# Queries loaded and turned first, w1 loaded ahead of an exchange, and two tiles of an expert begun early, in a fused attention and expert kernel

## The chip, the cores and the metric

The kernel runs on one core of a Trainium2 chip. The metric is the device time of one execution in microseconds; lower is better. Engines go by their names and by the short names of the profile: TensorE (PE), VectorE (DVE), ScalarE (ACT), GpSimd (POOL) and SyncE (SP).

## The reference

Two stages, one behind the other, in float32:

```python
def _attn_ref(q, k, v, sort_net):          # (4, 8, 768, 64) each; sort_net (4, 8, 8, 8)
    P = sort_net
    for _ in range(5):                     # exp, then rows and columns normalized
        P = P - np.max(P, axis=-1, keepdims=True)
        P = np.exp(P)
        P = P / (np.sum(P, axis=-1, keepdims=True) + 1e-09)
        P = P / (np.sum(P, axis=-2, keepdims=True) + 1e-09)
    k_sorted = np.einsum('bhij,bhjcd->bhicd', P, k_b)    # blocks of 96 rows mixed by P
    v_sorted = np.einsum('bhij,bhjcd->bhicd', P, v_b)
    scores = scale * np.matmul(q_b, k_sb.transpose(0, 1, 2, 4, 3))   # within each block
    attn = softmax(scores)
    return np.matmul(attn, v_sb)

def _moe_ref(x, w_gate, w1, w2):           # x (3072, 512), 8 experts, F = 1024
    P = np.exp(x @ w_gate - max)           # then balanced over rows and columns 8 times
    for e in range(8):
        out += P[:, e:e + 1] * (np.maximum(x @ w1[e], 0.0) @ w2[e])
```

The attention's output, with its heads side by side, is the x of the second stage.

## The kernel before, in words

The four batches of the attention are worked one after the other. While batch 1, 2 or 3 is in the attention, expert 0 runs on the tokens of the batch before it, woven between (`weave`). Behind the last batch come the balancing of the gates and experts 1 to 7, which fill most of the time. The part that the change touches is the opening: everything up to batch 0's attention, and the first tiles of expert 0.

**Loads.** `load_batch`, `load_rest`, `load_w1` and `load_w2` issue their DMAs from GpSimd (L75, L84, L89), which also turn float32 into bfloat16. They are issued in the order of the text: q, v and k of heads 0 to 3 of batch 0, the same of heads 4 to 7, v of batch 1 (768 KB in bfloat16), the gate's weights wg (L97). w1 and w2 of expert 0 and batch 1's k and q follow behind the exchange.

**The chain of P.** `sort_net` is loaded on SP (L60). Five rounds of one Exp on ACT (L118) and six or seven small instructions on DVE (L119 to L126) balance P. `Prep` (L130) is P repeated, which PE spreads over the partitions (L389), and DVE multiplies with a mask (L393) to the matrices R by which blocks are mixed.

**Batch 0.** `queries` turns the queries on PE (L178) and copies them on ACT (L190). `sort_values` multiplies v with R (L155), copies the result to vs (L157), and then exchanges partitions: eight DMAs of 97.5 KB (L165) take vs in SBUF to vsb in SBUF, one for each block. They are shared out over SP, ACT and GpSimd. Behind that, `attention` follows a written plan, in which a letter is a step and a digit a pair of heads:

```python
plan = ("k0 k1 w3 s0 q2 k2 w2 s1 q3 k3 d0 w1 s2 w2 d1 s3 d2 w1 m0 m1 d3 t0 v0 w1 m2 t1 "
        "w1 m3 t2 v0 w2 t3 l0 w3 l3" if first else
```

- q: `queries`. k: `keys`, the mixed keys (L200), copied on DVE (L205). s: `scores` (L219) and their Exp on ACT (L232).
- d: `denominators` (L243) and a reciprocal on DVE (L246). m: `mix`, attention times vsb (L255), multiplied with the reciprocals on DVE (L258). m0 is the first reader of vsb.
- t: `turn`, the output turned (L278) and copied to xtT, x turned (L281). l: `logits` with wg (L292), copied to glog (L296).
- v0: two heads of batch 1's `sort_values`. w with a digit: `warm`, so many matmuls (L381) into a bank of PSUM that nothing reads.

PSUM has seven banks here that go round, and one for the unread matmuls.

**Expert 0.** `expert` makes hidden tiles (L336, ReLU on ACT L338), eight for each chunk of 384 tokens, and then multiplies with w2 (L343). Batch 0's first chunk starts behind the plan's last step. Between its steps stand the other four heads of batch 1's `sort_values`, and behind these batch 1's exchange.

`pin` keeps instructions of an engine in the order of the text. A scheduler places those without it.

Of the kernel before, what the change touches and what calls it, by code (L numbers as in the profile page):

```python
# [25 lines left out]
def kernel(  # L26
# [31 lines left out]

    P = pp.tile([32, 8, 8], F32)
    nc.sync.dma_start(out=P, in_=sort_net.rearrange("b h i j -> (b h) i j"))  # L60

# [3 lines left out]
    def load_batch(bb, parts):  # L67
        for d, name in ((vt, "vt"), (kt, "kt"), (qt, "qt")):
            d[bb] = kvp.tile([128, 8, 384], BF16, name=name, bufs=2)
        load_rest(bb, parts)  # L70
# [19 lines left out]
                                in_=moe_w2[e].rearrange("(fb k) f -> k fb f", k=128)))  # L90

    Ibig = ones.tile([128, 128], BF16)
    make_identity(nc, Ibig)
    load_batch(0, [(x, l0, 4) for l0 in (0, 4) for x in "qvk"])
    load_batch(1, [("v", 0, 8)])
    wg = ones.tile([128, 4, E], BF16)
    pin(nc.gpsimd.dma_start(out=wg, in_=moe_w_gate.rearrange("(kk k) e -> k kk e", k=128)))  # L97
    mask16 = ones.tile([128, 16], F32)
    nc.vector.reduce_sum(out=mask16, in_=Ibig.rearrange("p (j c) -> p c j", c=16), axis=AX.X)

# [9 lines left out]
    rs = pp.tile([32, 8], F32)  # L110
    cs = pp.tile([32, 8], F32)
    Pt = P.rearrange("p i j -> p j i")
    nc.vector.reduce_max(out=rs, in_=P, axis=AX.X)
    nc.vector.tensor_sub(P, P, mkap(rs, [rs.ap[0], rs.ap[1], [0, 8]]))
    for it in range(5):


        nc.scalar.activation(out=P, in_=P, func=AF.Exp)  # L118
        nc.vector.reduce_sum(out=rs, in_=P, axis=AX.X)  # L119
        nc.vector.reciprocal(out=rs, in_=rs)  # L120
        nc.vector.tensor_mul(P, P, mkap(rs, [rs.ap[0], rs.ap[1], [0, 8]]))
        nc.vector.reduce_sum(out=cs, in_=Pt, axis=AX.X)
        if it == 0:
            nc.vector.tensor_scalar_add(cs, cs, 1e-9)
        nc.vector.reciprocal(out=cs, in_=cs)
        nc.vector.tensor_mul(Pt, Pt, mkap(cs, [cs.ap[0], cs.ap[1], [0, 8]]))  # L126

    Prep = perp.tile([32, 8, 8, 16], BF16)
    for eng, i0, n in ((nc.vector.tensor_copy, 0, 5), (nc.scalar.copy, 5, 3)):
        eng(Prep[:, i0:i0 + n], mkap(P, [P.ap[0], [8, n], [1, 8], [0, 16]], off=i0 * 8))  # L130

    xtT = xtp.tile([128, 4, N], BF16)
    osbl = xtp.tile([128, NT, Dm], F32)
    glog = xtp.tile([128, NT, E], F32)
    Pb = perp.tile([128, 32, 8], F32)
    Rt = {}

# [14 lines left out]
    def sort_values(bb, bank, n=8, h0=0):  # L152
        for h in range(h0, n):
            vps = bank([128, 384], F32)
            pin(nc.tensor.matmul(vps, Rt[bb][:, h].rearrange("p i c -> p (i c)"),  # L155
                                 vt[bb][:, h, :], start=True, stop=True))
            (nc.vector.tensor_copy if bb == 0 and h in (3, 5, 7) else nc.scalar.copy)(  # L157
                vs[:, :, h, 0:64], vps.rearrange("p (kk d) -> p kk d", d=64))
            if h % 2:
                yield  # L160

        for i in range(NB if n == 8 else 0):
            eng = ((nc.sync, nc.gpsimd, nc.scalar)[i % 3] if bb == 0 else
                   nc.gpsimd if i % 2 else nc.sync)
            (pin if bb == 0 else lambda ins: ins)(eng.dma_start(  # L165
                out=mkap(vsbt[bb % 2], [[VW, 96], [1, 520]], off=i * 520),
                in_=vs[16 * i:16 * i + 16].rearrange("p kk h d -> p kk (h d)")))
# [3 lines left out]
    def queries(bb, hp, bank):  # L171

        qps = bank([128, 6, 128], BF16)
        if bb < 2:

            for kk in range(6):
                for h in range(2):
                    pin(nc.tensor.matmul(qps[64 * h:64 * h + 64, kk, :],  # L178
                                         qt[bb][:, 2 * hp + h, kk * 64:kk * 64 + 64],
                                         Ibig, is_transpose=True, start=True, stop=True))  # L180
        else:
            qr = sp.tile([128, 6, 2, 64], BF16, name="qr", bufs=2)
            nc.gpsimd.tensor_copy(
                qr.rearrange("p kk h d -> p h kk d"),
                qt[bb][:, 2 * hp:2 * hp + 2].rearrange("p h (kk d) -> p h kk d", d=64))
            for kk in range(6):
                pin(nc.tensor.matmul(qps[:, kk, :], qr[:, kk].rearrange("p h d -> p (h d)"),  # L187
                                     Ibig, is_transpose=True, start=True, stop=True))
        qT[bb, hp] = sp.tile([128, 128, 6], BF16, name="qTs", bufs=4)
        nc.scalar.copy(qT[bb, hp], qps.rearrange("p kk c -> p c kk"))  # L190

    def keys(bb, hp, bank):

# [104 lines left out]
    def attention(bb, bank, values=None, warm=None):  # L298
        first = bb == 0

        def step(what, hp):
            if what == "q":
                queries(bb, hp, bank)
            elif what == "k":
                keys(bb, hp, bank)
            elif what == "s":
                scores(bb, hp, bank)
            elif what == "t":
                turn(bb, hp, bank, nc.scalar.copy if first and hp < 3 else nc.vector.tensor_copy)
            elif what == "l":  # L310
                logits(bb, bank, (0, 1, 2) if hp == 0 else (3,))
            elif what == "v":
                next(values, 0)
            elif what == "w":
                warm(hp)
            elif what == "d":
                denominators(hp, bank)
            else:
                for h in range(2):
                    mix(bb, hp, h, bank)  # L320

        plan = ("k0 k1 w3 s0 q2 k2 w2 s1 q3 k3 d0 w1 s2 w2 d1 s3 d2 w1 m0 m1 d3 t0 v0 w1 m2 t1 "
                "w1 m3 t2 v0 w2 t3 l0 w3 l3" if first else
                "q0,q1,k0 k1,s0,q2 k2,s1,q3 m0 k3,s2 m1,t0 s3 m2,t1 m3 t2 t3,l0 l3")
        for some in plan.split():
            for x in some.split(","):
                step(x[0], int(x[1]))
            yield


    def expert(e, c0, n, hsb, hbank, obank, done, hold):
        hTs = hsb()
        for fb in range(8):
            hps = hbank()
            for kk in range(4):
                hold(nc.tensor.matmul(hps[:, 0:n], w1t[e][:, kk, fb * 128:(fb + 1) * 128],  # L336
                                      xtT[:, kk, c0:c0 + n], start=(kk == 0), stop=(kk == 3)))
            nc.scalar.activation(out=hTs[:, fb, 0:n], in_=hps[:, 0:n], func=AF.Relu)  # L338
            yield
        for tt in range(n // 128):  # L340
            oacc = obank()
            for fb in range(8):
                hold(nc.tensor.matmul(oacc, hTs[:, fb, tt * 128:(tt + 1) * 128],  # L343
                                      w2t[e][:, fb, :], start=(fb == 0), stop=(fb == 7)))
                if fb == 3:
                    yield
            done(c0 // 128 + tt, oacc)
            yield
# [23 lines left out]
    with tc.tile_pool(name="ps0", bufs=7, space=bass.MemoryType.PSUM,  # L372
# [8 lines left out]
                pin(nc.tensor.matmul(unread, Ibig, mkap(Ibig, [Ibig.ap[0], [0, 4], [1, 128]]),  # L381
                                     start=True, stop=True))

        for hp in range(2):
            queries(0, hp, bank0)
        warm(9)
        pbps = bank0([128, 8, 32], F32)
        for i in range(8):
            pin(nc.tensor.matmul(pbps[:, i, :], Prep[:, i].rearrange("p j c -> p (j c)"),  # L389
# [10 lines left out]
        nc.scalar.copy(Pb, pbps.rearrange("p i g -> p g i"))  # L400
        half = build_r(1, nc.gpsimd, 4)
        next(half)
        load_w1(0)
        next(half, 0)
        load_w2(0)
        load_rest(1, [(x, l0, 4) for l0 in (0, 4) for x in "kq"])
        for _ in attention(0, bank0, sort_values(1, bank0, 4), warm):
            pass

    def weave(a, b, na, nb):  # L410
# [8 lines left out]
    with ExitStack() as c2:  # L419
# [4 lines left out]
        for bb in range(1, B):  # L424
            ex = expert0(bb - 1, lambda: mps.tile([128, 8, 384], BF16, name="hTs"),
                         ebank, ebank, pin)
            at1, left = attention(bb, bank1), 12 if bb == 1 else 26
            late = sort_values(1, bank1, 8, 4) if bb == 1 else iter(())
            for _ in range(28 - left):
                next(ex)  # L430
                next(late, 0)
            last = 3 if bb + 1 < B else 0
            left -= last
            cut = lambda k: left * k // 12
            weave(at1, ex, 5, cut(5))
            if bb + 1 < B:
                if bb == 2:
                    load_w1(1)
                load_batch(bb + 1, [(x, 0, 8) for x in "vkq"])
                for _ in build_r(bb + 1, nc.gpsimd, 4):  # L440
                    pass
                if bb == 2:
                    for _ in sum_w(1):
                        pass
            weave(at1, ex, 3, cut(8) - cut(5))
            if bb + 1 < B:
                weave(sort_values(bb + 1, bank1), ex, 5, last)
            weave(at1, ex, 4, left - cut(8))
            for _ in ex:
                pass  # L450
# [401 lines left out]
```

## Time and profile before

| | us |
|---|---|
| three timed executions | 675.99, 674.03, 676.01 |
| their median | 675.99 |
| the profiled execution | 674.6 |
| its span | 672.8 |
| PE busy in the span | 658.8 |
| HBM read, written | 52.45 MB, 6.29 MB |

The span runs from the first to the last instruction; 1.8 us of the profiled execution lie around it. All times in a view are counted from the span's start. Busy shares are those of the engines' queues, and a matmul's end in the timeline is modelled, so that matmuls overlap there; the start of the next group tells more than the length of one.

### The profile page before, as it was taken

The numbers are of one execution on the slowest core, as the hardware profiler recorded it, in microseconds if no ns is written. First come the engines' busy times: TensorE is split into PE (matmuls) and PEld (weight loads), VectorE is DVE, ScalarE is ACT, GpSimd is POOL, SyncE is SP. The second block draws the span as 40 slices with busy tenths as digits, with TensorE's granted clock in tenths as the row PEclk, the third lists the DMA queues.
The fourth block names the chain that finished last, engine by engine and source line by source line (L and its number), as shares of the span: only waits on it lengthen the run. The fifth ranks groups of instructions, "written<-read, shape, count | busy, mean of one in ns | idle before, by whom it ended". The sixth has DMA issues, their size and how long they took to land.

```text
span 672.8 us, 13418 instructions
## 1 busy us (share of the span) xinstructions
PE 658.8 (98%) x5185; PEld 436.0 (65%) x5185; DVE 470.2 (70%) x957; ACT 380.0 (56%) x738; POOL 470.0 (70%) x437
## 2 busy tenths in 40 slices
PE   5999999999999999999999999999999999999997
PEld 2756666654566666666666666666666666666665
DVE  6627646667677777777777777777777777777775
ACT  3656646466777755555555555555555555555540
POOL 4442651076979998779796979879787969846641
PEclk9999999999999999999999999999999999999999
DMA  9996872203040313030403040211303040000224
GB/s 154 195 221 102 155 123 33 33 1 63 1 64 3 62 10 55 1 63 0 64 1 63 1 63 2 37 28 12 53 0 63 1 64 1 1 1 35 92 86 166
DMA packets 31968, 36.57 MB, mean 54 GB/s; under 512 B 2016, under 2 KB 24384, under 8 KB 31904
## 3 DMA queue, kind: packets, MB, share of 16 engines
q0 software_dynamic: 26352, 27.72, 26.2%
q1 hardware_dynamic: 5328, 7.80, 3.6%
q8 instruction: 40, 0.66, 0.4%
q10 hardware_dynamic: 224, 0.20, 0.1%
q14 instruction: 24, 0.20, 0.1%
HBM read 52.45 MB, written 6.29 MB: 87 GB/s over the span
## 4 chain that ended last, share of the span: by engine, by line
PE 95%; DVE 2%; ACT 1%; issue 0%; DMA 0%; ACTq 0%; DVEq 0%
PE oacc L674 37%; PE bk L563 37%; PE bank L343 5%; PE bank L336 5%; PE bank L267 1%; PE bk L640 1%; PE oacc L739 1%; PE bank L219 1%; PE bank L200 1%; PE bank L278 1%; PE bk L731 1%; PE bank L155 1%; PE unread L381 1%; PE bk L739 1%; PE oacc L731 0%; PE bank L187 0%
## 5 line engine op out<-in xcount | busy, mean ns | idle before, releaser
L624 DVE SCALAR_TENSOR_TENSOR osbl<-oacc,glog,osbl 128x256 f32<-128x256 f32 (+1 forms) x410 | 219.1, 535 | 127.2 <-PE oacc L674 118.0
L549 ACT ACTIVATE hT<-bk 128x512 bf16<-128x512 f32 (+1 forms) x176 | 104.3, 592 | 148.6 <-PE bk L563 129.8
L563 PE MATMUL bk<-xtT,w1e 128*128 128x512 bf16 x504 | 149.1, 379 | 0.0
L674 PEld LDWEIGHTS <-hs 128*128 128x128 bf16 x984 | 96.2, 98 | 63.0 <-POOL hs L664 0.3
L674 PEld LDWEIGHTS <-hT 128*128 128x128 bf16 x904 | 88.4, 98 | 59.0 <-issue 1.8
L664 POOL TENSOR_TENSOR hs<-hT 128x512 bf16<-128x512 bf16 x82 | 94.9, 1157 | 36.5 <-DVE hT L552 31.1
L674 PE MATMUL oacc<-w2e,hT 128*128 128x256 bf16 x764 | 114.6, 273 | 0.3 <-DVE osbl L624 0.3
L664 POOL TENSOR_TENSOR hs<-hs,hT 128x512 bf16<-128x512 bf16 x82 | 94.8, 1156 | 6.4
L563 PE MATMUL bk<-xc,wc 128*128 128x512 bf16 x336 | 99.1, 379 | 0.1
L664 POOL TENSOR_TENSOR hs<-hT,hs 128x512 bf16<-128x512 bf16 x82 | 94.6, 1154 | 6.4
L674 PE MATMUL oacc<-w2e,hs 128*128 128x256 bf16 x616 | 92.4, 273 | 0.0
L563 PEld LDWEIGHTS <-w1e 128*128 128x128 bf16 x672 | 65.8, 98 | 11.7 <-issue 0.5
L552 DVE CUSTOM_DVE_ANT_0 hT<-bk,p 128x512 bf16<-128x512 f32 x84 | 58.1, 691 | 7.9 <-PE bk L563 3.1
L598 ACT COPY p<-bk 128x512 f32<-128x512 f32 x84 | 49.2, 586 | 24.8 <-PE bk L563 24.7
L592 ACT COPY u<-bk 128x512 f32<-128x512 f32 x84 | 49.3, 586 | 22.1 <-PE bk L563 22.0
L583 ACT COPY bk<-bk 128x512 f32<-128x512 f32 x84 | 48.0, 572 | 20.5 <-PE bk L563 20.5
L552 DVE CUSTOM_DVE_ANT_0 hT<-bk,u 128x512 bf16<-128x512 f32 x84 | 57.0, 679 | 1.0 <-PE bk L563 0.6
L674 PE MATMUL oacc<-w2s,hs 128*128 128x256 bf16 x368 | 55.2, 273 | 0.0
L563 PEld LDWEIGHTS <-wc 128*128 128x128 bf16 x504 | 49.3, 98 | 8.0 <-issue 0.2
L617 DVE SCALAR_TENSOR_TENSOR s<-bk,hT 128x512 bf16<-128x512 f32 x80 | 54.4, 680 | 0.0
L563 PE MATMUL bk<-xc,w1e 128*128 128x512 bf16 x168 | 50.0, 379 | 0.1
L563 PE MATMUL bk<-xtT,wc 128*128 128x512 bf16 x168 | 50.0, 379 | 0.0
(140 smaller groups left out, 853.0 us busy)
## 6 DMA issues: line engine op xcount, KB each, us to landing
w1e<-in_moe_w_dram POOLq DMA_DIRECT2D x8, 1024.0 KB, 8.1
w2e<-in_moe_w_dram POOLq DMA_DIRECT2D x8, 1024.0 KB, 8.9
out_dram<-osbl SPq DMA_DIRECT2D x23, 256.0 KB, 2.0
vt<-in_v_dram POOLq DMA_DIRECT2D x3, 768.0 KB, 11.9
qt<-in_q_dram POOLq DMA_DIRECT2D x4, 384.0 KB, 12.8
kt<-in_k_dram POOLq DMA_DIRECT2D x4, 384.0 KB, 13.4
kt<-in_k_dram POOLq DMA_DIRECT2D x2, 768.0 KB, 14.4
qt<-in_q_dram POOLq DMA_DIRECT2D x2, 768.0 KB, 16.5
```

What stands on the lines that cost most here:

```text
L336: hold(nc.tensor.matmul(hps[:, 0:n], w1t[e][:, kk, fb * 128:(fb + 1) * 128], xtT[:, kk, c0:c0 + n], start=(kk == 0), stop=(kk == 3)))
L343: hold(nc.tensor.matmul(oacc, hTs[:, fb, tt * 128:(tt + 1) * 128], w2t[e][:, fb, :], start=(fb == 0), stop=(fb == 7)))
L549: relu = lambda o, x: nc.scalar.activation(out=o, in_=x, func=AF.Relu)
L552: return nc.vector._custom_dve(TENSOR_ADD_SAT, out=o, in0=x, in1=y, s0=TOP, s1=0.0)
L563: pin(nc.tensor.matmul(ps, wa[:, kk, :], xa[:, kk, :], start=(first and kk == 0), stop=(kk == 1), skip_group_check=True))
L583: pin(nc.scalar.copy(t["w"], t["u"]))
L592: pin(nc.scalar.copy(t["u2"], t["u"]))
L598: pin(nc.scalar.copy(t["p5"], t["v"]))
L617: pin(nc.vector.scalar_tensor_tensor(out=s3[:, i, :], in0=t["w"], scalar=0.0, in1=c12, op0=ALU.max, op1=ALU.subtract))
L624: pin(nc.vector.scalar_tensor_tensor(out=o, in0=ps, scalar=glog[:, t, e:e + 1], in1=o, op0=ALU.mult, op1=ALU.add))
L664: pin(nc.gpsimd.tensor_tensor(out=s[:, c], in0=a, in1=b, op=o))
L674: pin(nc.tensor.matmul(ps, h[:, fb, :], w[:, fb, :], start=(first and fb == 0), stop=(fb == 3), skip_group_check=True))
```

## The change

It does the following.

- The first load is q of heads 0 to 3, ahead of the identity matrix `Ibig`; then q of heads 4 to 7, then v and k of heads 0 to 3 and of 4 to 7.
- w1 of expert 0 is loaded behind them, in the place of batch 1's v, which is now issued between the two parts of batch 1's R, behind the exchange.
- The gate's weights are loaded on SP as float32, behind `sort_net`, into a part of glog that is not in use yet, and a copy on GpSimd makes wg of them.
- All four pairs of heads of batch 0's queries are turned before P is ready, pinned between the Exps of the chain of P: two, then four unread matmuls, then the other two and three unread matmuls. Nine unread matmuls stood there.
- The exchange has four DMAs on SP, two on ACT and two on GpSimd. For batch 0 there were three, two and three.
- The plan of batch 0 has no q steps, ten unread matmuls where there were sixteen, m0 ahead of d2, and no steps of batch 1's `sort_values`. All eight heads of these now stand between expert 0's first tiles, with half of their copies on DVE.
- Steps e0, e1 and e2 (`begin`) make the first two hidden tiles of expert 0 inside the plan, a part of the contraction at a time, as the parts of xtT are done. `expert` leaves those two out.

```diff
+    wgf = glog[:, NT - 4:NT, :]
+    nc.sync.dma_start(out=wgf, in_=moe_w_gate.rearrange("(kk k) e -> k kk e", k=128))
...
+    load_batch(0, [("q", 0, 4)])
     make_identity(nc, Ibig)
-    load_batch(0, [(x, l0, 4) for l0 in (0, 4) for x in "qvk"])
-    load_batch(1, [("v", 0, 8)])
+    load_rest(0, [("q", 4, 4)] + [(x, l0, 4) for l0 in (0, 4) for x in "vk"])
+    load_w1(0)
     wg = ones.tile([128, 4, E], BF16)
-    pin(nc.gpsimd.dma_start(out=wg, in_=moe_w_gate.rearrange("(kk k) e -> k kk e", k=128)))
+    pin(nc.gpsimd.tensor_copy(wg, wgf))
...
-            (nc.vector.tensor_copy if bb == 0 and h in (3, 5, 7) else nc.scalar.copy)(
+            (nc.vector.tensor_copy if bb == 0 and h in (3, 5, 7) or bb == 1 and h % 2 else
+             nc.scalar.copy)(
...
-            eng = ((nc.sync, nc.gpsimd, nc.scalar)[i % 3] if bb == 0 else
-                   nc.gpsimd if i % 2 else nc.sync)
+            eng = (nc.sync if i % 2 == 0 else
+                   nc.scalar if bb == 0 and i % 4 == 1 else nc.gpsimd)
...
-        plan = ("k0 k1 w3 s0 q2 k2 w2 s1 q3 k3 d0 w1 s2 w2 d1 s3 d2 w1 m0 m1 d3 t0 v0 w1 m2 t1 "
-                "w1 m3 t2 v0 w2 t3 l0 w3 l3" if first else
+        plan = ("k0 k1 w3 s0 k2 w2 s1 k3 w2 d0 s2 d1 s3 w1 m0 d2 m1 d3 t0 m2 t1 m3 e0 t2 w2 t3 "
+                "l0 e1 l3 e2" if first else
...
+    def begin(bank, ks):
+
+        if not begun:
+            begun[0] = mps.tile([128, 8, 384], BF16, name="hTs")
+            begun[1] = [bank([128, 384], F32) for _ in range(2)]
+        for fb in range(2):
+            for kk in ks:
+                pin(nc.tensor.matmul(begun[1][fb], w1t[0][:, kk, fb * 128:(fb + 1) * 128],
+                                     xtT[:, kk, 0:384], start=(kk == 0), stop=(kk == 3)))
+            if 3 in ks:
+                nc.scalar.activation(out=begun[0][:, fb], in_=begun[1][fb], func=AF.Relu)
+
...
-        for hp in range(2):
-            queries(0, hp, bank0)
-        warm(9)
...
+            pin(nc.scalar.activation(out=P, in_=P, func=AF.Exp))
+            if it >= 2:
+                queries(0, it - 2, bank0)
+            if it == 3:
+                warm(4)
...
+        queries(0, 3, bank0)
+        warm(3)
...
-        load_w1(0)
+        load_batch(1, [("v", 0, 8)])
...
-        for _ in attention(0, bank0, sort_values(1, bank0, 4), warm):
+        for _ in attention(0, bank0, iter(()), warm):
...
-            late = sort_values(1, bank1, 8, 4) if bb == 1 else iter(())
-            for _ in range(28 - left):
+            late = sort_values(1, bank1) if bb == 1 else iter(())
+            for _ in range(28 - left - 2 * (bb == 1)):
```

More of the change, by code (lines that the diff above doesn't have):

```diff
@@ L60 @@
     nc.sync.dma_start(out=P, in_=sort_net.rearrange("b h i j -> (b h) i j"))
+    xtT = xtp.tile([128, 4, N], BF16)
+    osbl = xtp.tile([128, NT, Dm], F32)
+    glog = xtp.tile([128, NT, E], F32)
+    wgf = glog[:, NT - 4:NT, :]
+    nc.sync.dma_start(out=wgf, in_=moe_w_gate.rearrange("(kk k) e -> k kk e", k=128))
     pin = tc.keep_in_program_order
@@ L112 @@
     Pt = P.rearrange("p i j -> p j i")
[L113 to L126, printed above, removed]
-    Prep = perp.tile([32, 8, 8, 16], BF16)
[L129 to L134, printed above, removed]
+    Prep = perp.tile([32, 8, 8, 16], BF16)
     Pb = perp.tile([128, 32, 8], F32)
@@ L189, in queries @@
         qT[bb, hp] = sp.tile([128, 128, 6], BF16, name="qTs", bufs=4)
-        nc.scalar.copy(qT[bb, hp], qps.rearrange("p kk c -> p c kk"))
+        (pin if bb == 0 else lambda ins: ins)(
+            nc.scalar.copy(qT[bb, hp], qps.rearrange("p kk c -> p c kk")))
     def keys(bb, hp, bank):
@@ L317, in step @@
                 denominators(hp, bank)
+            elif what == "e":
+                begin(bank, ((0, 1), (2,), (3,))[hp])
             else:
@@ L328, in attention @@
             yield
+    begun = {}
+    def begin(bank, ks):
[8 more added lines that the diff above has]
+                nc.scalar.activation(out=begun[0][:, fb], in_=begun[1][fb], func=AF.Relu)
     def expert(e, c0, n, hsb, hbank, obank, done, hold):
-        hTs = hsb()
-        for fb in range(8):
+        hTs = begun[0] if c0 == 0 else hsb()
+        for fb in range(2 if c0 == 0 else 0, 8):
             hps = hbank()
@@ L382, in warm @@
                                      start=True, stop=True))
-        for hp in range(2):
-            queries(0, hp, bank0)
-        warm(9)
+        nc.vector.reduce_max(out=rs, in_=P, axis=AX.X)
+        nc.vector.tensor_sub(P, P, mkap(rs, [rs.ap[0], rs.ap[1], [0, 8]]))
+        for it in range(5):
+            pin(nc.scalar.activation(out=P, in_=P, func=AF.Exp))
[3 more added lines that the diff above has]
+                warm(4)
+            nc.vector.reduce_sum(out=rs, in_=P, axis=AX.X)
+            nc.vector.reciprocal(out=rs, in_=rs)
+            nc.vector.tensor_mul(P, P, mkap(rs, [rs.ap[0], rs.ap[1], [0, 8]]))
+            nc.vector.reduce_sum(out=cs, in_=Pt, axis=AX.X)
+            if it == 0:
+                nc.vector.tensor_scalar_add(cs, cs, 1e-9)
+            nc.vector.reciprocal(out=cs, in_=cs)
+            nc.vector.tensor_mul(Pt, Pt, mkap(cs, [cs.ap[0], cs.ap[1], [0, 8]]))
+        for eng, i0, n in ((nc.vector.tensor_copy, 0, 5), (nc.scalar.copy, 5, 3)):
+            (pin if i0 else lambda ins: ins)(
+                eng(Prep[:, i0:i0 + n], mkap(P, [P.ap[0], [8, n], [1, 8], [0, 16]], off=i0 * 8)))
+        queries(0, 3, bank0)
+        warm(3)
         pbps = bank0([128, 8, 32], F32)
```

## The prediction

> **What bounds the kernel now.** I read the page first, then the timeline of the first 60 us, the chain of waits, the DMA issues one by one, and the windows. The page:
>
> ```profile
> span 672.8 us, 13418 instructions
> PE 658.8 (98%) x5185; PEld 436.0 (65%) x5185; DVE 470.2 (70%) x957; ACT 380.0 (56%) x738; POOL 470.0 (70%) x437
> ```
>
> TensorE (PE) is busy 98% of the span. From 33 us on its idle stretches are short, so whatever PE finishes earlier up to there reaches the end, and nothing else does. The change touches only the first 40 us. The timeline (start, length, engine, line):
>
> ```profile
> 10.36 0.15 PEld L381 LDWEIGHTS <-Ibig 128*128 128x128 bf16 x1 [0.28 <-issue]
> 10.79 0.15 PEld L381 LDWEIGHTS <-Ibig 128*128 128x128 bf16 x1 [0.28 <-issue]
> 11.11 0.10 PEld L381 LDWEIGHTS <-Ibig 128*128 128x128 bf16 x1 [0.18 <-issue]
> ...
> 12.92 0.36 PE L389 MATMUL bank<-Ibig,Prep 32*128 32x32 bf16 x8 [1.22 <-DVE Prep L130]
> ...
> 17.93 0.53 PE L178 MATMUL bank<-Ibig,qt 128*64 128x128 bf16 x12
> ...
> 25.30 1.59 PE L255 MATMUL bank<-vsb,atp 96*96 96x88 bf16 x32
> ...
> 33.28 0.81 PE L336 MATMUL bank<-xtT,w1e 128*128 128x384 bf16 x4
> ...
> 39.13 5.34 PE L343 MATMUL bank<-w2e,hTs 128*128 128x512 bf16 x24
> ```
>
> Until 12.9 us PE only waits for the chain of P on VectorE and ScalarE (Prep, L130). From there it is nearly gapless, but part of what it runs is unread matmuls (L381). Two marks serve below: the first mix at 25.30 (m0, L255, reads vsb) and the first w2 matmul at 39.13. The unread ones start every 0.43 us until about 11.0 us and then faster; in the chain of waits (start, length, what) they take 0.22 us:
>
> ```profile
> 20.26 0.46 PE bank L178 x12
> 32.62 0.67 PE unread L381 x3
> 35.07 0.33 PE bank L155 x2
> 35.39 3.90 PE bank L336 x24
> ```
>
> So PE runs at half rate until about 11 us; the PEclk column reads 1.00 throughout and does not show it. The DMA issues, asked one at a time (KB, then us to landing; in order k's second half, v of batch 1, the exchange's first and last piece on SP, w1):
>
> ```profile
> kt<-in_k_dram POOLq DMA_DIRECT2D x1, 384.0 KB, 11.1
> vt<-in_v_dram POOLq DMA_DIRECT2D x1, 768.0 KB, 14.4
> vsb<-vs SPq DMA_DIRECT2D x1, 97.5 KB, 4.6
> vsb<-vs SPq DMA_DIRECT2D x1, 97.5 KB, 6.8
> w1e<-in_moe_w_dram POOLq DMA_DIRECT2D x1, 1024.0 KB, 11.7
> ```
>
> With the issue times (5.31, 6.04, 16.52, 17.9, 19.71) they land at 16.4, 20.4, 21.1, 24.7 and 31.4. The windows (PE, PEld, DVE, ACT, POOL busy, PEclk, DMA share, GB/s) say why:
>
> ```profile
> 5.00:15.00 10.00, 6.96 (x51) 3.62 (x52) 7.62 (x32) 3.45 (x9) 2.72 (x4) 1.00 1.31 203
> 15.00:19.00 4.00, 3.80 (x71) 2.30 (x69) 3.66 (x8) 2.49 (x7) 1.88 (x4) 1.00 1.32 204
> 21.00:22.00 1.00, 1.00 (x22) 0.81 (x17) 0.99 (x2) 1.00 (x4) 1.00 (x2) 1.00 1.06 293
> ```
>
> DMA is saturated at 203 GB/s by the GpSimd queue from 5 us. The exchange, issued from 16.5, moves nothing before 19 us and its first piece lands only after v of batch 1 did. It is complete 0.6 us before m0 needs it.
>
> **The change, part by part.** *Chain of P.* Order of instructions: on VectorE the mask reduction (L99, 0.36 us) now stands between a column sum and its reciprocal inside the third iteration; before, it ran at 6.84 while VectorE waited for an Exp. Cost about 0.3 on the path (0 if it slips, 0.4 at most). On ScalarE three copies of turned queries (0.77 each) now stand behind Exps; the wait for VectorE there is 1.55 us per iteration, so they are covered as long as q's first half lands before about 7.5. It landed at 6.8 and is issued 0.7 earlier (ahead of the identity, 0.74 instead of 1.46). If it came later than 7.5, the Exp behind the copy, and all of P, would slip by as much. w_gate moves to SP behind P's load, where nothing follows until the exchange; its cast on GpSimd stands ahead of two exchange issues and waits for a load that is long done. Zero.
>
> *Removed from PE between 12.9 and 39.1.* 24 transposes (0.36 + 0.42 by start times; now done while PE waits for P): 0.8. Unread matmuls of the attention plan 16 to 10: 6 x 0.22 = 1.3. Nine unread ahead of P's matmuls become four plus three: beside the wait for Prep, 0. Gaps of PE between 17 and 34 that the early expert matmuls may fill: 0.3. Four v matmuls (0.65) move behind, eight expert matmuls (1.3) move ahead of the last logits: both stay before 39.13, 0. Upper bound of the gain: 0.8 + 1.3 + 0.3 - 0.3 = 2.1 us.
>
> *When m0 can start.* On PE alone: 25.30 less 0.8 (transposes), 0.65 (three unread), 0.74 (the denominators d2, now behind m0), plus 0.3: 23.4. Exps on ScalarE, back to back from 18.25 to 25.88 with two copies (about 0.6 each) among them, end near 25.0; only d3, later, needs the last. But the exchange now stands behind w1 instead of v. w1 follows k's second half: 15.7 (0.7 earlier), plus 1024 KB, 5.2 us at 203 GB/s or 6.3 at the 167 GB/s of 72 to 79 us, where another w1 load runs: landing 20.9 to 22.0, against 20.7 for w_gate's, last in that queue before the exchange. So the exchange is 0.2 to 1.3 later, 0.75 in the middle; w_gate's small rows no longer stand in the queue, some 0.5 back. Last piece 24.7 + 0.25 = 24.95; as it is read seventh of eight (0.045 apart), m0 behaves as if it began at 24.65. PE idles there about a microsecond: the unread matmuls and transposes that went were partly cover for this wait, and d2, which could fill it, is queued behind m0.
>
> *From m0 to 39.13.* Before: 13.8 us. After: five unread fewer (1.1), d2 more (0.74): 13.5, and VectorE's eight products (0.62 each) leave no more to win. The gain is 25.30 - 24.65 + 0.3 = 0.95, say 1.0.
>
> *Later covers.* w2 landed at 36.5 (21.56 + 14.9), needed at 39.1 and now 38.1; the queue has the same bytes ahead of it. q of batch 1 landed at 45.7 (24.73 + 21.0), needed at 48.5, now 47.5. v of batch 1 comes about 29, needed about 33. Its copies, half now on VectorE, run beside PE.
>
> [...] The row: the exchange's SP piece took 4.6 us, and P's load, alone, 1.7. [...]
>
> **Rivals.**
> - A, the forecast: m0 waits a little for the exchange; gain 1.0.
> - B, the exchange is not held: it lands before 23.7 and m0 starts at 23.4; gain 1.9 + 0.3, held to the upper bound of 2.1: 672.5. For it: only two pieces remain behind w1 on GpSimd's queue. Against: the 4.6 us.
> - C, slower: v of batch 1, issued about 19.4, is served while SP's four pieces wait, so the last ones come a v load later (4.0 us by 16.4 to 20.4). Landing 21.5 + 4.0 and two pieces of about 1 us: 27.6, m0 at 27.3; loss 1.7, 676.3. It turns to a loss when the last piece lands after 25.9. For it: SP now has four pieces in a row. Against: w1 behind the old exchange did not hold it so long.
> - D, the clock: PE comes to P's matmuls at half rate, since 9 unread in a row became 4, transposes, 3. Four unread then cost 0.86 more, eight v matmuls 1.3 more; with the rest hidden by VectorE some 2 us later, so a net loss of about 1.0: 675.6. Against: transposes began the busy stretch before too, and PE was fast 4.2 us after they began.
> - E, nothing: 674.6; a later wait (w2, q) takes it all back.
>
> [...]
>
> **How the numbers follow.** The sum is made against the profiled execution, 674.6 (span 672.8 and 1.8 around it): 673.6. The four executions shown (674.0, 674.6, 676.0, 676.0) average 675.2, 0.6 above it; I add half of that: 673.9. The median of before is 675.99, and 0.3% of it, about what a measurement of this kernel can tell from no change, is 2.0, itself the spread of before. So A falls on both sides of the bound 673.96. Chances: A 0.46 (0.24 faster, 0.21 same, 0.01 slower), B 0.24 (0.22, 0.02, 0), C 0.14 (0, 0.08, 0.06), D 0.11 (0, 0.07, 0.04), E 0.05 (0.01, 0.04, 0). Sums: faster 0.47, same 0.42, slower 0.11. Range: B's 672.5 less the 0.6 by which the lowest run of before is under its profiled one, 671.9, to C's 676.3 plus the 1.4 by which the median of before exceeds its profiled run, 677.7; 677.5 leaves little out.
>
> **What would show it.** After: the first matmul on queries near 6.1; unread loads 0.43 or 0.22 apart at 11 to 13.5; Prep's matmuls at 13.2; m0 at 23.4 to 24.7 with a PE wait on vsb of about 1 us in it; first w2 matmul at 38.1. A wait on vsb past 25.6, unread matmuls 0.43 apart behind 13.2, or a w2 matmul at 37 prove the sum wrong.

## The result, and the profile after

The changed kernel took 682.39 us (median of six executions, 680.24 to 684.2), the kernel before, run beside it, 675.55 (674.03 to 676.01): a ratio of 1.0107, 95% interval 1.0083 to 1.013. It is slower, and above the range of the prediction. The profiled execution of after took 683.73, with a span of 681.6; before it was 674.6 with 672.8. The same two lines of the page:

```profile
span 681.6 us, 13333 instructions
PE 658.6 (97%) x5100; PEld 439.7 (65%) x5177; DVE 472.9 (69%) x961; ACT 379.0 (56%) x734; POOL 469.2 (69%) x436
```

PE is busy for as long as before (658.8), but 8.8 us are added to the span. The timeline of PE says where (start, length, engine, line; in brackets the idle time ahead and what ended it):

```profile
6.62 1.49 PE L164 MATMUL bank<-Ibig,qt 128*64 128x128 bf16 x24 [6.62 <-DMA qt<-in_q_dram]
...
12.84 0.36 PE L410 MATMUL bank<-Ibig,Prep 32*128 32x32 bf16 x8 [0.16 <-DVE Prep L405]
13.13 1.04 PE L384 MATMUL unread<-Ibig 128*128 128x512 bf16 x4
...
16.16 0.81 PE L140 MATMUL bank<-vt,R 128*128 128x384 bf16 x4 [1.34 <-DMA vt<-in_v_dram]
...
27.12 0.24 PE L242 MATMUL bank<-vsb,atp 96*96 96x88 bf16 x2 [1.41 <-DMA vsb<-vs]
29.14 0.93 PE L242 MATMUL bank<-vsb,atp 96*96 96x88 bf16 x10 [1.77 <-DMA vsb<-vs]
...
46.81 3.40 PE L346 MATMUL bank<-w2e,hTs 128*128 128x512 bf16 x14
```

m0 (L242) comes to vsb at 24.6, stands (waits with nothing else to run) 3.7 us in four waits, and is released for good at 29.14, where before it began at 25.30: 3.84 us later. The other mark, the first w2 matmul, moved from 39.13 to 46.81: 7.68 later. So as much again was lost behind m0, where PE does not stand at all. The windows behind m0 (PE, PEld, DVE, ACT, POOL busy, then PEclk), three of after and the middle one of before, name it:

```profile
25.00:30.00 5.00, 1.45 (x18) 1.21 (x17) 0.53 (x1) 0.98 (x3) 1.42 (x2) 0.92 1.26 217
30.00:35.00 5.00, 5.00 (x67) 5.00 (x66) 2.63 (x6) 0.41 (x1) 0.00 (x0) 0.50 1.26 206
35.00:40.00 5.00, 5.00 (x53) 4.07 (x52) 2.65 (x4) 1.57 (x3) 0.00 (x0) 0.56 1.32 203
```

```profile
30.00:35.00 5.00, 4.89 (x69) 3.37 (x67) 2.19 (x5) 2.81 (x7) 0.00 (x0) 1.00 1.25 208
```

PEclk, the clock granted to PE as a share of full rate, fell to 0.50. The trace's record of the clock has 10.24 us at half rate, from 29.2 to 39.4; in the profiled execution of before it stays at full from about 11 us to the end of the work. Another 0.3 us are added between 47 and 139 us, and 0.79 by a wait of PE for POOL at 210 us.

What released m0 is in the chain of waits (start, length, what):

```profile
4.96 11.06 DMA vt<-in_v_dram
...
17.80 0.70 SPq L151
...
19.43 2.64 SPq L151
...
22.11 6.98 DMA vsb<-vs
```

The exchange starts at 17.80 (before 16.52), since v's second half landed at 16.02 (before 14.57). SP's four issues follow one another; the third takes 2.64 us, so the fourth piece goes out at 22.11 and lands 6.98 us later, at 29.09. The pieces on ACT and GpSimd had all landed by 25.2.

So there are two losses: the late last SP piece, and the clock behind it. The experiments take them apart.

### The profile page after: what moved, and what is told of

It is laid out like the page before. It is cut to its first block, busy times and chain, and to the rows that moved or that the text cites. A ratio compares the mean times of both kernels' runs of the same rounds, so it can differ in the third digit from the quotient of the medians.

```text
span 681.6 us, 13333 instructions
## 1 busy us (share of the span) xinstructions
PE 658.6 (97%) x5100; PEld 439.7 (65%) x5177; DVE 472.9 (69%) x961; ACT 379.0 (56%) x734; POOL 469.2 (69%) x436
## 4 chain that ended last, share of the span: by engine, by line
PE 81%; POOL 8%; DMA 5%; issue 2%; DVE 1%; ACT 1%; SPq 1%; DVEq 0%; POOLq 0%; ACTq 0%
PE oacc L695 33%; PE bk L584 30%; PE bank L346 5%; PE bank L339 4%; POOL hs L685 4%; DMA vt<-in_v_dram 2%; DMA w2e<-in_moe_w_dram 1%; PE bank L254 1%; DMA w1e<-in_moe_w_dram 1%; POOL wc L372 1%; POOL w2s L512 1%; DMA vsb<-vs 1%; PE bk L661 1%; PE bank L265 1%; PE bk L752 1%
## 5 line engine op out<-in xcount | busy, mean ns | idle before, releaser
L584 PE MATMUL bk<-xtT,w1e 128*128 128x512 bf16 x478 | 143.5, 379 | 0.9
L584 PE MATMUL bk<-xc,wc 128*128 128x512 bf16 x317 | 95.2, 379 | 0.1
L584 PE MATMUL bk<-xtT,wc 128*128 128x512 bf16 x160 | 48.2, 379 | 0.4
L584 PE MATMUL bk<-xc,w1e 128*128 128x512 bf16 x158 | 47.8, 379 | 0.1
## 6 DMA issues: line engine op xcount, KB each, us to landing
vsb<-vs SPq DMA_DIRECT2D x16, 97.5 KB, 4.5
```

The source lines that it names most:

```text
L584: pin(nc.tensor.matmul(ps, wa[:, kk, :], xa[:, kk, :], start=(first and kk == 0), stop=(kk == 1), skip_group_check=True))
```

## The experiments

### The standing and the clock

**e1_cover.** Only the plan of after is changed, so that unread matmuls fill the wait ahead of m0:

```diff
-k3 w2 d0 s2 d1 s3 w1 m0 d2
+k3 w2 d0 s2 d1 s3 w9 w9 m0 d2
```

> The changed kernel, with 18 unread matmuls in the place of the one ahead of m0 (3.9 us of TensorE work at full rate), so that TensorE works through most of the wait for the exchange. Theory 1 (the late exchange leaves TensorE idle, and the idle stretch halves its clock for about 10 us): m0's last piece still arrives near 29, but the granted clock stays 1.0 from 25 to 40, and the first w2 matmul comes 3 to 4 us earlier, near 43: 678 to 679.5 against 682.4. Theory 2 (the loss is the wait for the exchange alone, the half clock is hidden behind VectorE): 682, as the changed kernel. Theory 3 (the clock falls because there are fewer unread matmuls in the whole plan, wherever they stand): between, a short half-rate stretch stays.

677.32 us (676.99 to 677.78), ratio 1.0038 [1.0025, 1.0052]. PE's timeline:

```profile
23.77 4.06 PE L384 MATMUL unread<-Ibig 128*128 128x512 bf16 x18
27.67 0.87 PE L242 MATMUL bank<-vsb,atp 96*96 96x88 bf16 x16
```

PEclk reads 1.00 in every window from 20 to 45 us, here from 30 to 35:

```profile
30.00:35.00 5.00, 4.99 (x103) 4.32 (x102) 3.81 (x8) 2.40 (x3) 0.00 (x0) 1.00 1.27 207
```

5 us of the loss are gone, more than was expected, for two reasons. The first w2 matmul is at 41.19, 13.52 behind m0; in after that stretch took 17.67. So 4.15 us are the price of the clock. And m0 begins 1.47 earlier than after's last release: the last piece landed at 27.05, though it was expected near 29 and the loads are the same as after's. The end of the exchange thus differs by 2 us between two executions with the same loads.

**e2_share** and **e6_share_unread.** e2 shares the exchange as before (three pieces on SP, three on GpSimd, two on ACT), e6 adds unread matmuls to that, 17 in its plan where after has 10 (not 19, as its expectation counts), five of the seven ahead of m0:

```diff
-            eng = (nc.sync if i % 2 == 0 else
-                   nc.scalar if bb == 0 and i % 4 == 1 else nc.gpsimd)
+            eng = ((nc.sync, nc.gpsimd, nc.scalar)[i % 3] if bb == 0 else
+                   nc.gpsimd if i % 2 else nc.sync)
...
-k3 w2 d0 s2 d1 s3 w1 m0 d2 m1 d3 t0 m2 t1 m3 e0
+k3 w2 d0 w2 s2 w2 d1 w1 s3 w1 m0 d2 m1 d3 t0 w1 m2 t1 w1 m3 e0
```

The last two lines are e6's alone.

> The changed kernel with the exchange of batch 0 shared out as before: three pieces on SyncE, three on GpSimd, two on ScalarE. Theory 1a (the fourth piece on SyncE's queue is what comes last, since its issue is held 2.6 us): the last piece lands near 27 instead of 29.1, TensorE's idle stretch shortens to about 2.5 us, the clock may stay at 1.0: 676 to 680. Theory 1b (w1 ahead in the GpSimd queue holds all of the exchange, however it is shared out): last piece still 28 to 29, 681 to 683.

> The changed kernel with the old sharing of the exchange (three pieces on SyncE) and nine more unread matmuls in the plan, 19 in all, in or near the places where they stood before. It asks whether the half clock comes from the wait of TensorE alone or from too few dense matmuls around it. Theory 3 (the density counts): granted clock 0.997 to 1.0 in all runs, 674.5 to 676. [...]

e2: 677.96 (675.06 to 680.41), ratio 1.0042 [1.002, 1.0063]. e6: 675.21 (674.72 to 675.92), 1.001 [1.0, 1.0019]. e2's ten executions fall into groups by their mean clock: four at 0.999 to 1.0 took 675.1 to 676.1, three at 0.994 to 0.995 took 677.7 to 678.5, three at 0.990 to 0.992 took 679.9 to 680.4. e6's are all at 0.998 or more. e2's profiled execution:

```profile
24.57 0.29 PE L242 MATMUL bank<-vsb,atp 96*96 96x88 bf16 x3 [0.43 <-DMA vsb<-vs]
25.14 0.60 PE L242 MATMUL bank<-vsb,atp 96*96 96x88 bf16 x10 [0.28 <-DMA vsb<-vs]
```

The exchange is complete at 25.09 (18.42 and 6.67), earlier than either theory put it, and m0 stands 0.9 us in three pieces. All the same the clock falls at 27.2 us and stays at half for 6.83; sixteen mix matmuls at 28.78 take 1.45 us, where those at 26.29 took 0.89. With the unread matmuls of e6 PE stands 0.25 us and the clock stays, but their work takes what the change had removed: first w2 matmul at 39.11.

**e8_before_ten_unread.** The plan of before with ten unread matmuls, in the places where after has them (the plans are shown from k3 on).

```diff
-k3 d0 w1 s2 w2 d1 s3 d2 w1 m0 m1 d3 t0 v0 w1 m2 t1 w1 m3 t2 v0 w2 t3 l0 w3 l3
+k3 w2 d0 s2 d1 s3 w1 d2 m0 m1 d3 t0 v0 m2 t1 m3 t2 v0 w2 t3 l0 l3
```

> The kernel before with ten unread matmuls in the plan instead of sixteen, at the places where the changed kernel has them; loads, exchange and queries as before. Theory 3 (too few dense matmuls alone let the clock fall): mean clock 0.990 to 0.996, 677 to 680. Theory 1 (without a wait for the exchange nothing happens): TensorE reaches m0 about 0.6 us earlier, about as the last piece lands; clock as before, 673.5 to 674.8.

674.87 (673.24 to 675.79), ratio 1.0004 [0.9994, 1.0014]; no wait on vsb, and the clock holds. Fewer unread matmuls alone did no harm here. They gained nothing either: m0 begins 0.57 earlier, at 24.73, but PE then stops for 1.27 us, for which the profile names no cause, and the first w2 matmul is at 39.15.

```profile
31.18 0.20 PE L278 MATMUL bank<-Ibig,og 96*128 96x96 bf16 x1 [1.27 <-issue]
```

So in these runs the clock fell behind a wait for vsb (0.9 us in e2), and not for want of unread matmuls alone (e8 has a PEclk of 1.00 in every window from 5 to 45 us). But e1 and e6 do not tell the standing from a lack of dense work, since unread matmuls fill the one and supply the other.

In after's record of the clock the full rate ahead of the fall lasted 17.07 us, from 12.1 to 29.2, and the half rate 10.24. In the other kernels that lost the clock the half rate behind the standing lasted 6.83, 10.24, 13.65 or 17.07 us, which are to each other as 2, 3, 4 and 5. How long PE stood for vsb in the profiled execution, and how long the clock was then at half:

| kernel | PE stood, us | half rate, us |
|---|---|---|
| e9 | 4.1 | 13.65 |
| e3 | 3.8 | 17.07 |
| after | 3.7 | 10.24 |
| e5 | 3.7 | 10.24 |
| e4 | 2.0 | 10.24 |
| e10 | 1.9 | 10.24 |
| e7 | 1.4 | 6.83 |
| e15 | 1.3 | 6.83 |
| e12 | 1.1 | 10.24 |
| e2 | 0.9 | 6.83 |
| e16 | 0.7 | 0 |
| e14 | 0.6 | 0 |
| e6 | 0.25 | 0 |

In e2 0.9 us of standing was enough. The length of the standing does not settle it, though. The table holds for the profiled executions alone: e12's is one of two among nine that lost the clock, and e16's one of two among six that kept it. Waits for other things count too: e13 stood 3.45 us for w1 and e11 2.0 us for v of batch 1, and each lost 6.83. But the 1.27 us of e8 left the clock at full (PEclk 1.00 from 30 to 40 us), and behind waits of up to 1.5 us for Prep (e13) PEclk was 1.00 from 15 to 20; behind e11's 1.75 us there it was 0.79 in that window. What else decides is not shown.

### What makes the last piece late

**e3_v_first** puts v of batch 1 back ahead of the exchange and w1 behind it, as in before (steps e0 to e2 stand at the end of the plan, since w1 is later); four pieces stay on SP. **e7_before_four_on_sp** is the kernel before with after's sharing line alone.

```diff
e3:
-    load_w1(0)
+    load_batch(1, [("v", 0, 8)])
...
-        load_batch(1, [("v", 0, 8)])
+        load_w1(0)
e7:
-            eng = ((nc.sync, nc.gpsimd, nc.scalar)[i % 3] if bb == 0 else
-                   nc.gpsimd if i % 2 else nc.sync)
+            eng = (nc.sync if i % 2 == 0 else
+                   nc.scalar if bb == 0 and i % 4 == 1 else nc.gpsimd)
```

> The changed kernel with the old order of the two large loads: v of batch 1 ahead of the exchange, w1 behind it; the begun tiles of expert 0 stand at the end of the plan, since w1 now lands later. Theory 1b (w1 ahead of the exchange is the cause): the exchange lands near 25 to 26, m0 waits at most 1.5 us, no half clock: 675 to 677. Theory 1a (four pieces on SyncE): the last piece still lands near 28, 680 to 683.

> The kernel before with only the sharing of the exchange taken from the changed kernel: four pieces on SyncE, two on ScalarE, two on GpSimd. Theory 1a (the fourth piece on SyncE comes last because its issue is held): last piece near 27 to 28, m0 waits 2 to 3 us, the clock falls in most runs: 678 to 683. Theory 1b (w1 ahead of the exchange, or the late v, is needed for the loss): under 676.

e3: 684.95 (683.84 to 685.63), ratio 1.0147 [1.013, 1.0163], above both expectations; the last piece lands at 28.1. That w1 stands ahead of the exchange is not the cause. e7: 679.36 (677.79 to 680.83), ratio 1.0068 [1.0042, 1.0095]. One changed line in before gives more than half of the loss, by both steps: m0 waits 1.37 us for a piece issued at 18.67 (below, from its chain), and PEclk is 0.80 from 25 to 30 us and 0.51 from 30 to 35.

```profile
18.67 8.49 DMA vsb<-vs
```

But why is a fourth piece on SP slow? Two theories stood: the queue of loads ahead of the exchange, or the load behind it.

**e9_quiet, e10_quiet_share, e11_quiet_before** take away what stands ahead. e9 is after with w1 issued behind the exchange; e10 the same with e2's sharing; e11 is before with v of batch 1 behind the exchange.

```diff
     load_rest(0, [("q", 4, 4)] + [(x, l0, 4) for l0 in (0, 4) for x in "vk"])
-    load_w1(0)
...
         half = build_r(1, nc.gpsimd, 4)
+        load_w1(0)
         next(half)
         load_batch(1, [("v", 0, 8)])
e11, against before:
-    load_batch(1, [("v", 0, 8)])
...
         half = build_r(1, nc.gpsimd, 4)
+        load_batch(1, [("v", 0, 8)])
         next(half)
         load_w1(0)
```

> After, with w1 of expert 0 issued behind the exchange (then v of batch 1, w2, k and q), so that GpSimd's queue has nothing left when the exchange is issued; SyncE still has four of the eight pieces. Theory B (backlog): the pieces on SyncE are late because they share the transfer engines with a GpSimd queue that is full. Then the last piece lands at 22 to 23.5 with four on SyncE too, no fourth issue is held for over 1 us, m0 waits under 0.5 us, the clock stays at 1.00, and the time is 673 to 676; w1 and w2 land some 5 us later and may add up to 2. Rival I (the issues): four issues in a row on SyncE are slow by themselves. Then the fourth piece is again issued near 22 and lands at 26 or later, m0 waits over 1 us, the granted clock falls to 0.5 to 0.6 behind it, and the time is 678 to 683.

> The same as the run with w1 behind the exchange, and the exchange shared as before: three pieces on SyncE, three on GpSimd, two on ScalarE. Theory B: last piece at 22 to 23, no wait on vsb, clock 1.00, 673 to 675.5, the same as with four on SyncE within 0.3%. Rival I: 3 us or more faster than with four on SyncE. If w1 and w2, which land later, make expert 0's first tiles wait, both are 1 to 3 us above this, and the waits stand at the first w1 or w2 matmuls.

> Before, with v of batch 1 issued behind the exchange, ahead of w1. Theory B: the exchange is complete near 22 where before it was at 24.7; m0 was not waiting in before, so nothing is gained there, and w1, w2, k and q come no earlier: 674 to 676.5, the same as before. Rival I: the pieces on SyncE land as before, 24 to 25.

e9: 684.14 (683.7 to 684.88), ratio 1.0138 [1.0118, 1.0157]. e10: 681.95 (680.71 to 682.56), 1.0102 [1.0081, 1.0123], 2.2 below e9 and so between its two expectations. e11: 680.73 (679.24 to 681.9), 1.0084 [1.0056, 1.0113]. The theory of the queue ahead fell: e9's chain ends

```profile
19.32 0.64 SPq L150
...
20.00 9.14 DMA vsb<-vs
```

at 29.14, although its first SP piece took only 3.2 us. Its transfers between 24 and 27 us, by queue (packets, MB, share of 16 engines), are GpSimd's, which is w1, and SP's, which is the rest of the exchange:

```profile
q0 software_dynamic: 212, 0.43, 91.4%
q1 hardware_dynamic: 137, 0.13, 15.9%
```

SP's last two pieces share the transfer engines with the next load and get a quarter of the bytes. e11 lost its time in another place: v of batch 1 landed at 31.3, where step v0 of before's plan needs it; PE stood 2.0 us there and the clock fell for 6.83 us. Its exchange was late too, since PE came out of P at half rate (PEclk 0.79 from 15 to 20 us), and with nothing ahead it took 8.1 us from the first issue on SP to the last landing, where before takes 8.2.

**e12_hold, e13_hold_all** take the load behind away: GpSimd reads one element of each block of vsb before it issues v of batch 1, w2, k and q. e13 puts w1 there too, so that nothing stands ahead either.

```diff
         next(half)
-        load_batch(1, [("v", 0, 8)])
         next(half, 0)
+        held = pp.tile([1, 8], BF16)
+        pin(nc.gpsimd.tensor_copy(held, mkap(vsbt[0], [[VW, 1], [520, 8]])))
+        load_w1(0)          # e13 alone, and not ahead of the exchange
+        load_batch(1, [("v", 0, 8)])
         load_w2(0)
```

> After, with w1 still ahead of the exchange and four pieces on SyncE, but GpSimd issues no load behind the exchange before all eight pieces have landed (a small read of vsb on GpSimd stands ahead of v of batch 1; both halves of batch 1's R are made before it). Theory L (load behind): the last SyncE pieces are late because the next load on GpSimd's queue is served beside them. Then the last piece lands at 24.5 to 26, the standing of m0 falls from 3.7 us to 0.5 to 1.8, and the time is 675 to 679. Rival F (queue in front): the backlog ahead of the exchange and the held fourth issue make it. Then the last piece still lands at 27 or later and the time is 680 to 684.

> The same with w1 too behind the landed exchange: nothing ahead of the exchange on GpSimd's queue and nothing beside it, four pieces on SyncE. Theory L: the last piece lands at 22 to 23.7, before m0 is reached, no wait on vsb, clock 1.00 up to there; the first w1 matmul (37) may wait for w1, which lands at 29 to 33, not at all; w2 lands near 42 and may cost up to 3 us at the first w2 matmul: 674 to 678. Rival I (four issues on one queue are slow by themselves): last piece at 26 or later, 679 or more.

e12: 675.71 (675.25 to 679.64), ratio 1.0021 [1.0009, 1.0032], as theory L expects. Seven of its nine executions took 675.25 to 676.29, where after's six took 680.24 to 684.2: holding the load back takes most of the loss away. In its profiled execution the fourth SP piece goes out at 19.34 and takes 6.3 us:

```profile
vsb<-vs SPq DMA_DIRECT2D x1, 97.5 KB, 6.3
```

With a load behind, a fourth piece comes late in one of two ways. In e3, e4, e5, e7 and e9 it goes out by 20.8, but takes 7.2 to 9.1. In after and e1 the third issue is held, for 2.64 and 1.65 us; the fourth goes out at 22.11 and 20.66 and takes 7.0 and 6.4. What holds that issue, no run shows.

e13: 680.13 (679.09 to 681.2), 1.0083 [1.007, 1.0096]. Its last piece lands at 23.39, as theory L expects, so four issues in a row are not slow by themselves, and PE does not stand for vsb. But its time misses the range. Its chain has the fourth piece and then the price of holding w1, for which PE stands 3.45 us at step e0:

```profile
19.24 4.15 DMA vsb<-vs
...
24.04 8.10 DMA w1e<-in_moe_w_dram
```

From the first issue on SP to the last landing of the exchange, in us, one profiled execution each:

| pieces on SP | a load behind | none behind |
|---|---|---|
| four | after 11.3, e1 9.7, e3 10.8, e4 9.6, e5 10.7, e7 10.6, e9 11.5 | e12 8.6, e13 6.6 |
| three | before 8.2, e2 8.3, e6 8.7, e8 7.7, e10 9.0, e11 8.1 | e14 7.9 |

e4, e5 and e14 follow below. With four pieces, every exchange with a load behind took 9.6 or more, and the two without 8.6 or less. Nothing stands ahead of the exchange in e9, e10, e11 and e13. Beside the spread that changes nothing where a load follows; where none does, the load ahead costs about 2 (e12 less e13). With three pieces on SP the load behind costs nothing that shows.

### Can the removed work show?

**e14_hold_share** is e12 with e2's sharing (the diffs of both). **e15_one_queue** is after with all eight pieces on GpSimd's queue, between w1 and v, and **e16_one_queue_w4** adds three unread matmuls to that.

```diff
-            eng = (nc.sync if i % 2 == 0 else
-                   nc.scalar if bb == 0 and i % 4 == 1 else nc.gpsimd)
+            eng = nc.gpsimd if bb == 0 or i % 2 else nc.sync
e16 also:
-d1 s3 w1 m0 d2
+d1 s3 w4 m0 d2
```

> The run that holds the loads behind the exchange (w1 ahead of it), with three pieces on SyncE, three on GpSimd and two on ScalarE. Theory L: last piece at 23.5 to 24.7, m0 stands under 0.7 us, the clock stays at 1.00 if PE's pauses are that short, first w2 matmul at 38 to 39: 673 to 675.5. If three pieces on SyncE with v loaded beside them (677.96) were only late by the issue, no change from that: 677 to 678.5.

> After, with all eight pieces of the exchange on GpSimd's queue, between w1 and v of batch 1, so that no load can be served beside them and no read of vsb is needed to hold it. Eight issues of 0.54 us: the last goes out near 21.5. Theory L: the last piece lands at 24 to 25.3, m0 stands 0.3 to 1.5 us, w2 lands by 36 and costs no wait; first w2 matmul 38.1 to 39; 673 to 675.5 where the clock holds, 676 to 678.5 where it falls behind m0's standing. Rival: GpSimd's queue itself is the slow part; then pieces land past 27 and the time is above 679.

> The same with four unread matmuls ahead of m0 where one stood (0.66 us of PE, in time that PE otherwise stands). If short standing with little work ahead of m0 is what lets the clock fall, every run has a clock of 0.996 or more, and the time is 673.5 to 675.5; if not, it spreads as without them.

e14: 675.97 (675.19 to 680.09), ratio 1.0037 [1.0022, 1.0052]. Its profiled execution keeps the clock:

```profile
24.64 0.99 PE L242 MATMUL bank<-vsb,atp 96*96 96x88 bf16 x13 [0.58 <-DMA vsb<-vs]
...
39.07 5.35 PE L346 MATMUL bank<-w2e,hTs 128*128 128x512 bf16 x24 [0.63 <-DMA w2e<-in_moe_w_dram]
```

The last piece landed at 24.99, 0.3 later than expected, and the median is 0.5 above the range. Here the sum of the prediction can be seen at work: PE is ready for w2 at 38.44, 0.7 before the old mark, and then waits for w2, whose load was held. Four of its twelve executions have a clock of 0.994 or less and take 677.7 to 680.1; the other eight take 675.2 to 676.8.

e15: 679.85 (678.84 to 680.14), ratio 1.007 [1.0056, 1.0084], the time of the rival, though no piece came past 27. The eighth issue on GpSimd had to wait until w1 had landed (idle time in brackets), so the last piece came at 26.4:

```profile
23.32 0.52 POOL L150 DMA_DIRECT2D vsb<-vs  x1 [1.83 <-DMA w1e<-in_moe_w_dram]
```

e16: 678.61 (675.11 to 680.1), 1.0052 [1.0033, 1.0072]. Its expectation failed: three more unread matmuls cut the standing to 0.7 us in the profiled execution, and only two of six executions kept the clock. How long PE may stand before the clock falls stays open.

### The opening

**e4_gate** loads the gate's weights on GpSimd again, behind w1; **e5_order** loads v's first half between the halves of q.

```diff
e4:
-    nc.sync.dma_start(out=wgf, in_=moe_w_gate.rearrange("(kk k) e -> k kk e", k=128))
...
-    pin(nc.gpsimd.tensor_copy(wg, wgf))
+    pin(nc.gpsimd.dma_start(out=wg, in_=moe_w_gate.rearrange("(kk k) e -> k kk e", k=128)))
e5:
-    load_rest(0, [("q", 4, 4)] + [(x, l0, 4) for l0 in (0, 4) for x in "vk"])
+    load_rest(0, [("v", 0, 4), ("q", 4, 4), ("k", 0, 4), ("v", 4, 4), ("k", 4, 4)])
```

> The changed kernel with w_gate loaded as before, by GpSimd as bfloat16, now behind w1. Asks why v's second half came 1.5 us later (16.1 instead of 14.6). Theory G (the small rows of the gate's load on SyncE disturb the first loads): v's second half lands near 14.5, the exchange is issued near 16.5, and the whole gets 1 to 2 us faster: 680 to 681.5. Theory Q (two loads of q in a row run slower than loads of different tensors): nothing changes before 16 us, and the small rows stand ahead of the exchange's two GpSimd pieces: 682 to 683.5.

> The changed kernel with v's first half loaded between the two halves of q. Theory Q (two loads of q in a row are what makes DMA slower between 5 and 10 us, 163 instead of 202 GB/s): v's second half lands by 14.7, its matmuls wait less than 0.3 us, the exchange is issued near 16.5 and m0 ends 1.0 to 1.5 us earlier; the clock may still fall, 679 to 682. Theory S (the first load's earlier start, alone or with the identity's instructions between, leaves the engines unequal): v's second half still lands at 15.5 to 16, 682.

e4: 682.27 (676.93 to 684.21), ratio 1.0098 [1.0069, 1.0128], v's second half still at 15.8. The gate's load does not delay it. One of its six executions kept the clock (0.999) and took 676.93; the other five, at 0.990 to 0.992, took 682.13 to 684.21. e5: 683.35 (680.49 to 684.08), 1.0118 [1.0092, 1.0145]: v's second half came at 15.0 and DMA moved 196 GB/s from 5 to 10 us (after 163, before 202), but q's second half came later, at 11.0 (after 10.2), PE and ACT with it, and PE was still at half rate at 15.89 (unread matmuls 0.42 us apart). So the exchange was issued at 18.45, and neither expectation held. The earlier v suggests the order of the loads without settling it: in the other kernels made from after, the second half took 10.1 to 11.1 us from its issue, in those made from before 9.6 to 10.0.

No version tried beats the kernel before. The nearest are e8 and e6.

## Why the prediction was wrong, point by point

- **The opening of the P chain: right in kind.** The mask reduction was to cost 0.3; Prep's matmuls came at 12.84 (before 12.92), so it cost nothing. q's first half was put at 6.1 and came at 6.6, still ahead of the 7.5 at which it would have held P. Its issue moved from 1.46 to 1.26, 0.2 and not 0.7 earlier.
- **The loads behind it: missed.** The working let v's second half land as before. It was 1.45 us later, PE stood 1.34 for it, and the exchange was issued 1.28 later. In the other kernels with the same order of loads it was 0.4 to 1.3 later, so after's profile shows the worst of it. k's second half, put at 15.7, landed at 17.96, and w1, put at 20.9 to 22.0, at 23.39.
- **PE's own work: right, in part by luck.** From m0 to the first w2 matmul 13.5 was forecast, and e1, at full clock, has 13.52. PE alone was to reach m0 at 23.4; it came at 24.6, and less the 1.34 for v that is 23.3. But two terms of that 23.4 were wrong and nearly cancel: the plans have nine and eight unread matmuls ahead of m0, so one went (0.22) and not three (0.65), and the 0.3 for the mask was not paid.
- **The exchange's last piece: the step that failed first.** The term said 0.25 behind before's 24.7, so 24.95. It was 29.09. In e1, with the same loads, it was 27.05, so the miss is 2.1 to 4.1. In after the larger part of it is a late issue: the fourth piece went out at 22.11, where e12's went out at 19.34 and landed at 25.65. The sum priced the exchange as one block behind w1 and took over the landing of three pieces on SP for four. With three, e2 has 25.09. That this is so near 24.95 is luck: w1 landed at 22.66 there, 1.9 behind before's last load ahead of the exchange (20.73), where the sum allowed 0.2 to 1.3.
- **Rival C had the mechanism, at least in part**, with a chance of 0.14 and too low a price. It had v of batch 1 served while SP's pieces wait, a last piece at 27.6 and a loss of 1.7. e9, e12 and e13 show that the load behind delays the last pieces; that it also holds the third issue, as happened in after, is not shown. What spoke against it, that w1 behind the old exchange did not hold it so long, overlooked that the old exchange had only three pieces on SP: e7, with four, is held by that same w1. Its 27.6 lies among the measured 27.05 (e1), 27.18 (e4) and 29.09 (after). Its price lacked the clock.
- **Rival B did not come: the sharing cost time.** That the exchange would not wait for w1 was counted as a gain, with the last piece before 23.7; in after it landed at 29.09. In e9 SP's last pieces do not wait for the load to land, but move beside it: 137 packets of SP's and 212 of GpSimd's in 3 us, GpSimd's about 2 KB each and SP's about 1. The fourth piece took 9.14 us there, and 4.15 in e13, where no load follows until the exchange has landed.
- **The clock behind a wait: the step that failed second, a term that was not there.** "PE idles there about a microsecond" was priced as a microsecond. In e2's profiled execution such a microsecond brought 6.83 us of half rate. In after the clock cost 17.67 less 13.52, so 4.15 us. The three terms give the mark: 3.84 for m0, 4.15 for the clock, less 0.31 of PE work saved, 7.68.
- **Rival D looked for the clock in the wrong place.** The four unread matmuls behind Prep's take 0.22 us each, full rate (the line at 13.13 above). Transposes and few unread matmuls at P did no harm in after. In e5, where q's second half came late, PE did come to P's matmuls at half rate, as D had it: the same four, from 14.21 to 15.89, take 0.42 each.

The forecast's answer to its own test stands: "a wait on vsb past 25.6" was named as what would prove the sum wrong, and 27.12 and 29.14 did.

## What to carry to other kernels

Price a DMA that something waits for by the last piece on each queue and by what is issued behind it, not only by what stands ahead: in e9 the last pieces shared with the next load and got 0.13 of 0.56 MB. Price a wait of TensorE ahead of a stretch that it bounds not by its own length alone but also by the clock that it may lose: in e2 6.83 us at half rate followed 0.9 us of standing, and in after the clock cost 4.15 us. And an unread matmul that looks like waste may be the cover of such a wait, as in e1 and e6, where PEclk stayed at 1.00: remove it only where the wait goes as well.

## What the runs showed of the hardware that was not expected

- Half-rate stretches of 6.83 (e2), 10.24 (after), 13.65 (e9) and 17.07 us (e3), to each other as 2, 3, 4 and 5, followed standings of PE as short as 0.9 us, while 0.6 and 0.7 us (e14, e16), and 1.27 us in e8, left the clock alone in the profiled executions. Executions of one kernel differ with the clock by over 5 us (e2: 675.06 to 680.41).
- The same four 97.5 KB pieces on one SP queue need 6.6 us from first issue to last landing in e13 and 11.5 in e9, where a 1 MB load is issued on another queue before the fourth.
- With w1 still in transfer, GpSimd's queue took seven pieces and held the eighth for 1.8 us until w1 had landed (e15, and the same in e16).
